# A fused attention and two-layer kernel: weight splits of layer 1 moved from GpSimd to ScalarE and VectorE, a buffer of its own for parked weights, and sums written from PSUM straight to x's two parts

## The chip, the cores and the metric

The kernel runs on one core of a Trainium2 chip. The metric is device time in microseconds (us) of one execution; lower is better. Before the change, three runs gave 705.80, 707.14 and 709.77 us, median 707.14. The core has five engines that run side by side, each in its own program order: TensorE (PE in the profile, its weight loads PEld), VectorE (DVE), ScalarE (ACT), GpSimd (POOL) and SyncE (SP), which here issues the DMAs.

## The reference, cut to what matters

```python
def reference(q, k, v, w_pre, w_post, moe_*, moe2_*):      # 2 x 12 heads x 448 x 64
    x = attention with head mixing before and after softmax  # -> [896, 768]
    h = x @ w_in                       # layer 1: [896, 768] @ [768, 2048]
    g = h * clip(h + 3, 0, 6) / 6
    x = g @ w_out                      # [896, 2048] @ [2048, 768]
    h = x @ w_in2                      # layer 2, the same sizes
    P = a0 + a1*h + a2*h^2 + a3*h^3
    Q = 1 + |b0|*|h| + |b1|*h^2
    return (P / (Q + 1e-6)) @ w_out2   # [896, 768]
```

[...]

## The kernel before, in words

**Exactness by splitting.** Every factor of a product is split in two float32r parts, a high part (rounded to what TensorE multiplies) and a low part (the rest): x = xh + xl, w = wh + wl. One product is then three matmuls, wh·xh, wh·xl and wl·xh, added up in the same PSUM bank (`mm3`, lines 387 to 389). Much of what the other engines do is to make these parts.

**Stages.** First the attention, whose order is written out by hand. Then layer 1's first product, called h here: 16 values of f (128 columns of w_in each), for each f two parts of the tokens (384 and 512 columns, `PARTS`), 6 x 3 matmuls each. `act1` makes g from h: ScalarE t (L561), VectorE g (L563), ScalarE the high part gh (L565), VectorE the low part gl (L566). Then layer 1's second product, called y: 6 blocks c of 128 rows; each needs all 16 gh and gl, and w_out in three units of 6, 6 and 4 values of f (`KSP`); two PSUM banks for a block, out of eight. At a block's end ScalarE copies y/6 from PSUM to a temporary buffer (L775), VectorE rounds it to XH (L776) and subtracts for XL (L777). XH and XL are the x of layer 2. Layer 2 is built alike, with other act functions. From the end of layer 1's first steps on (line 723) a scheduler sets the order on each engine, from the order of the code and from when it takes buffers to come free.

**Weights, unit by unit.** `advance` loads raw weights up to two units ahead (SP's queue, L426, into two wraw buffers) and splits one unit ahead. `split_pieces` takes a unit through: ScalarE scales the upper halves to float (L435), VectorE shifts (L437), puts in the sign (L439) and the lower bits (L443); this gives wf, of which there are two buffers. Then the high part wh and the low part wl, three buffers each. For the units of layer 1 ("in1" and "out1") GpSimd makes both (L459, L460); for those of layer 2 ScalarE makes wh (L462) and VectorE wl (L463).

**Parked weights.** For ten values of f of layer 2's w_in (2 to 11), `pre_slot` does the conversion already during layer 1 and parks the result in DRAM. It takes turns of three slots: load raw (L744), convert (into a wf buffer, with the same four steps L435 to L443), store (L752). Layer 2 later only loads the float (L411).

Of the kernel before, what the change touches and what calls it, by code (L numbers as in the profile page):

```python
# [7 lines left out]
F32 = mybir.dt.float32  # L8
F32R = mybir.dt.float32r
I32 = mybir.dt.int32  # L10
AF = mybir.ActivationFunctionType
ALU = mybir.AluOpType
# [36 lines left out]
def fused_kernel(  # L49
# [15 lines left out]
    nc = tc.nc  # L65
# [44 lines left out]
    XH = xp.tile([128, KD, NT], F32R, name="xh")  # L110
    XL = xp.tile([128, KD, NT], F32R, name="xl")
# [49 lines left out]
    for i, w in enumerate((w_pre, w_post)):  # L161
        nc.sync.dma_start(
            out=wrep[:, i, :], in_=w[None, :, :].to_broadcast([GR, H, H])
# [220 lines left out]
    pools = {}  # L384

    def mm3(o, wh, wl, mh, ml, first, last):
        nc.tensor.matmul(o, lhsT=wh, rhs=mh, start=first, stop=False)  # L387
        nc.tensor.matmul(o, lhsT=wh, rhs=ml, start=False, stop=False)  # L388
        nc.tensor.matmul(o, lhsT=wl, rhs=mh, start=False, stop=last)  # L389

    KSP = [(0, 6), (6, 12), (12, 16)]
    units = [("in1", f, 0) for f in range(KF)]
# [55 lines left out]
    def split_pieces(u):  # L448
        t, n = raws.pop(u)
        n *= 128  # L450
        if u[0] == "in2" and u[1] in pre:
            w = t
        else:
            w = pools["late"].tile([128, KD * 128], F32, tag="wf", bufs=2, name="wf")[:, :n]
            yield from to_f32(t, n, w)
        hv = pools["late"].tile([128, KD * 128], F32R, tag="wh", bufs=3, name="wh")[:, :n]
        lv = pools["late"].tile([128, KD * 128], F32R, tag="wl", bufs=3, name="wl")[:, :n]
        if u[0] in ("in1", "out1"):
            nc.gpsimd.tensor_scalar(out=hv, in0=w, scalar1=1.0, scalar2=0.0, op0=ALU.mult, op1=ALU.add)  # L459
            nc.gpsimd.tensor_tensor(out=lv, in0=w, in1=hv.bitcast(F32), op=ALU.subtract)  # L460
        else:
            nc.scalar.activation(out=hv, in_=w, func=AF.Copy)  # L462
            nc.vector.tensor_tensor(out=lv, in0=w, in1=hv.bitcast(F32), op=ALU.subtract)  # L463
        if u[0] == "out2":
            for d, x in zip(wsp[u[1]], (hv, lv)):
                nc.sync.dma_start(out=d, in_=x.bitcast(F32))
        else:
            hv, lv = (x.rearrange("p (a b) -> p a b", b=128) for x in (hv, lv))
        spl[u] = (hv, lv)
# [15 lines left out]
    def advance(i, ahead=2):  # L485
        load_units(i + ahead)
        split_units(i + 1)
# [60 lines left out]
            pass  # L548

    def tmp(name, n):  # L550
        return pools["gp"].tile([128, 512], F32, tag="tmp", bufs=4, name=name)[:, :n]

    def act1(f, p):
        t0, t1 = PARTS[p]
# [157 lines left out]
    gp = pools["gp"] = tc.alloc_tile_pool(name="gp", bufs=1, reuse_waits="tile")  # L712
# [15 lines left out]
    def bank(name):  # L728
        return pm.tile([128, 512], F32, tag="mm", name=name)
# [3 lines left out]
    slot, held = [0], {}  # L733

    def pre_slot():
        i, k = divmod(slot[0] - 1, 3)
        slot[0] += 1
        if not 0 <= i < len(PRE2):
            return
        f = PRE2[i]  # L740
        n = KD * 128
        if k == 0:
            held["t"] = gp.tile([128, 2 * n], I32, tag="wpre", name=f"wpre{f}")
            nc.sync.dma_start(  # L744
                out=held["t"].rearrange("p (a b) -> p a b", b=256), in_=w2i[:, :, f * 256 : f * 256 + 256]
            )
        elif k == 1:
            held["w"] = pools["late"].tile([128, n], F32, tag="wf", bufs=2, name="wf")
            for _ in to_f32(held["t"], n, held["w"]):
                pass  # L750
        else:
            nc.sync.dma_start(out=pre[f], in_=held["w"])  # L752
# [9 lines left out]
    for c in range(KD):  # L762
        hp = [bank(f"y1_{c}_{p}") for p in range(2)]
        for kk, (k0, k1) in enumerate(KSP):
            advance(ui)
            wh, wl = spl.pop(("out1", c, kk))
            for f in range(k0, k1):
                for p, (t0, t1) in enumerate(PARTS):
                    mm3(hp[p][:, : t1 - t0], wh[:, f - k0, :], wl[:, f - k0, :], gh[f][:, t0:t1], gl[f][:, t0:t1],
                        f == 0, f == KF - 1)  # L770
            pre_slot()
            ui += 1
        for p, (t0, t1) in enumerate(PARTS):
            y = tmp("y", t1 - t0)
            nc.scalar.activation(out=y, in_=hp[p][:, : t1 - t0], func=AF.Copy, scale=1.0 / 6.0)  # L775
            nc.vector.tensor_copy(out=XH[:, c, t0:t1], in_=y)  # L776
            nc.vector.tensor_tensor(out=XL[:, c, t0:t1], in0=y, in1=XH[:, c, t0:t1].bitcast(F32), op=ALU.subtract)  # L777
    pm.release()
    gp.release()

# [2 lines left out]
    gp = pools["gp2"] = tc.alloc_tile_pool(name="gp2", bufs=1, reuse_waits="tile")  # L783
# [57 lines left out]
    for f in range(KF):  # L841
        advance(ui, AHEAD2)
        w = spl.pop(("in2", f, 0))
# [8 lines left out]
        hp = hps[0]  # L852
        run(gemms[0])
        t1 = tm("t1", P0)
# [3 lines left out]
        if f == 0:  # L858
            hp = hps[1]
            run(gemms[1])  # L860
        else:
            hp = bank2(tags[1], f"h2_{f}_1")
# [55 lines left out]
    for t in range(NB0):  # L918
        o = gp.tile([TB, DM], F32, tag="o", bufs=3, name=f"o0_{t}")
# [15 lines left out]
    for t in range(NB1):  # L935
        row = P0 + t * TB
        o = gp.tile([TB, DM], F32, tag="o", bufs=3, name=f"o1_{t}")
# [61 lines left out]
```

## Time and profile before

| what | us |
|---|---|
| median of three runs | 707.14 |
| the profiled execution's own time | 707.37 |
| its span, first to last instruction | 705.7 |
| TensorE busy | 689.6 |
| VectorE busy | 557.2 |
| ScalarE busy | 411.1 |
| GpSimd busy | 256.9 |
| mean granted TensorE clock | 0.998 of full speed |

All rows below come from that one profiled execution; it lies within the three runs. Times in it count from the start of the span. A busy TensorE is one with a matmul on the way; matmuls overlap, so two starts can be closer together than a matmul is long. What TensorE really takes for a matmul is read from one start to the next.

### The profile page before, as it was taken

How to read it: one execution, taken by the hardware profiler on the slowest of the kernel's cores; microseconds unless marked ns; L12 is line 12 of the kernel's file. 1: busy time of each engine (PE TensorE's matmuls, PEld its weight loads, DVE VectorE, ACT ScalarE, POOL GpSimd, SP SyncE). 2: the span in 40 equal slices, each digit the busy share in tenths (PEclk: the TensorE clock that was granted, in tenths of full speed). 3: DMA queues.
4: the chain of work that ended last, by engine and by line, in shares of the span. 5: the costliest groups of instructions: out<-in, count | busy, mean ns of one | idle time of the engine just before them, and what ended most of it. 6: DMA issues, size and time to landing. Idle time of an engine off the chain costs nothing.

```text
span 705.7 us, 12410 instructions
## 1 busy us (share of the span) xinstructions
PE 689.6 (98%) x4461; PEld 617.5 (88%) x4461; DVE 557.2 (79%) x934; ACT 411.1 (58%) x851; POOL 256.9 (36%) x255
## 2 busy tenths in 40 slices
PE   8989999999999999999999999999999999999997
PEld 4768888888889888989888888889999999999997
DVE  6845585665657689889987777879999899989991
ACT  6757887887787343434342212227766667679851
POOL 2876775877776334323434543410000000000000
PEclk9999999999999999999999999999999999999999
DMA  5636486545394444555345544466575584755522
GB/s 206 226 111 176 142 209 190 166 142 166 119 260 123 148 144 136 155 157 156 121 151 177 186 160 141 140 247 236 209 270 186 196 267 144 242 196 202 188 82 89
DMA packets 76032, 122.81 MB, mean 174 GB/s; under 512 B 6804, under 2 KB 56260, under 8 KB 75972
## 3 DMA queue, kind: packets, MB, share of 16 engines
q1 hardware_dynamic: 75684, 121.66, 53.9%
q8 instruction: 35, 0.57, 0.3%
q10 hardware_dynamic: 288, 0.37, 0.1%
q14 instruction: 25, 0.20, 0.1%
HBM read 83.39 MB, written 19.27 MB: 145 GB/s over the span
## 4 chain that ended last, share of the span: by engine, by line
PE 60%; DVE 24%; DMA 7%; ACT 4%; issue 4%; POOL 0%; POOLq 0%; SPq 0%; ACTq 0%; DVEq 0%
PE A L341 9%; DVE wf L439 6%; PE h L389 6%; PE h L388 6%; PE h L387 6%; DVE wf L443 6%; PE acc L387 6%; PE acc L389 6%; PE acc L388 6%; PE X L363 5%; DMA pre<-wf 4%; PE sc L271 4%; DVE gl L566 4%; PE M L306 3%; DVE wf L437 3%
## 5 line engine op out<-in xcount | busy, mean ns | idle before, releaser
L389 PE MATMUL h<-xh,wl 128*128 128x512 f32 (+1 forms) x384 | 139.9, 364 | 0.8 <-DVE wl L463 0.8
L388 PE MATMUL h<-xl,wh 128*128 128x512 f32 (+1 forms) x384 | 139.5, 363 | 0.0
L387 PE MATMUL h<-xh,wh 128*128 128x512 f32 (+1 forms) x384 | 139.5, 363 | 0.0
L435 ACT ACTIVATE wf<-wraw 128x768 f32<-128x768 f32 (+1 forms) x56 | 48.7, 878 | 96.0 <-DMA pre<-wf 57.2
L296 POOL TENSOR_TENSOR sl<-full,sh 120x448 fp32r<-120x448 f32 x87 | 99.9, 1148 | 7.2
L310 DVE TENSOR_REDUCE st<-M 120x1 f32<-120x448 f32 x90 | 56.1, 623 | 51.3 <-PE M L308 51.1
L341 PEld LDWEIGHTS A<-wr,e 120*112 120x112 f32 x720 | 87.2, 178 | 7.9 <-ACT wr L325 3.9
L341 PE MATMUL A<-wr,e 120*112 120x120 f32 x720 | 89.7, 268 | 2.2 <-ACT wr L325 2.2
L459 POOL TENSOR_SCALAR wh<-wf 128x768 fp32r<-128x768 f32 (+1 forms) x34 | 32.6, 959 | 141.4 <-DVE wf L443 140.5
L312 ACT ACTIVATE e<-M,st 120x448 f32<-120x448 f32 x90 | 57.1, 635 | 42.7 <-DVE st L310 37.1
L389 PEld LDWEIGHTS h<-xh,wl 128*128 128x128 f32 x384 | 72.0, 188 | 9.0 <-DVE wl L463 1.1
L387 PEld LDWEIGHTS h<-xh,wh 128*128 128x128 f32 x384 | 72.1, 188 | 7.5
L388 PEld LDWEIGHTS h<-xl,wh 128*128 128x128 f32 x384 | 72.1, 188 | 7.6
L389 PE MATMUL y<-gh,wl 128*128 128x384 f32 x192 | 70.1, 365 | 2.6 <-POOL wl L460 2.6
L388 PE MATMUL y<-gl,wh 128*128 128x384 f32 x192 | 70.2, 366 | 1.0 <-DVE gl L566 1.0
L294 POOL TENSOR_SCALAR sh<-full 120x448 fp32r<-120x448 f32 x87 | 54.3, 624 | 46.1 <-PE M L307 21.5
L387 PE MATMUL y<-gh,wh 128*128 128x384 f32 x192 | 69.9, 364 | 0.0
L460 POOL TENSOR_TENSOR wl<-wf,wh 128x768 fp32r<-128x768 f32 (+1 forms) x34 | 67.5, 1985 | 2.8
L439 DVE SCALAR_TENSOR_TENSOR wf<-wraw,icst,wf 128x768 int32<-128x768 int32 (+1 forms) x56 | 61.7, 1103 | 0.7
L437 DVE TENSOR_SCALAR wf<-wf 128x768 int32<-128x768 int32 x66 | 43.1, 654 | 22.6 <-ACT wf L435 22.3
L443 DVE SCALAR_TENSOR_TENSOR wf<-wraw,icst,wf 128x768 int32<-128x768 int32 (+1 forms) x56 | 57.7, 1032 | 0.6
L565 ACT ACTIVATE gh<-g 128x384 fp32r<-128x384 f32 (+1 forms) x32 | 18.5, 579 | 60.3 <-DVE g L563 60.0
(114 smaller groups left out, 1521.7 us busy)
## 6 DMA issues: line engine op xcount, KB each, us to landing
wraw<-in_moe_w_out_dram SPq DMA_DIRECT2D x28, 768.0 KB
wraw<-in_moe_w_in_dram SPq DMA_DIRECT2D x22, 768.0 KB
full<-stg SPq DMA_DIRECT2D x60, 210.0 KB
vraw<-in_v_dram SPq DMA_DIRECT2D x42, 224.0 KB
wpre<-in_moe_w_in_dram SPq DMA_DIRECT2D x10, 768.0 KB
w2h<-wh SPq DMA_DIRECT2D x16, 384.0 KB
w2l<-wl SPq DMA_DIRECT2D x16, 384.0 KB
ws<-w2h SPq DMA_DIRECT2D x16, 384.0 KB
```

Of the source, the lines that this page charges most:

```text
L294: eng.tensor_scalar(out=sh[:r], in0=s[:r], scalar1=1.0, scalar2=0.0, op0=ALU.mult, op1=ALU.add)
L296: return lambda: eng.tensor_tensor(out=sl[:r], in0=s[:r], in1=sh[:r].bitcast(F32), op=ALU.subtract)
L310: nc.vector.tensor_reduce(out=st[:r, 0:1], in_=mt[:r, :S], op=ALU.max, axis=AX.X, negate=True)
L312: nc.scalar.activation(out=e[:r], in_=mt[:r, :S], func=AF.Exp, bias=st[:r, 0:1], accum_out=st[:r, 1:2])
L341: nc.tensor.matmul(av[:, jc], lhsT=e[:r, jc * JP : (jc + 1) * JP], rhs=wr[:r, :, :rr], start=True, stop=True)
L387: nc.tensor.matmul(o, lhsT=wh, rhs=mh, start=first, stop=False)
L388: nc.tensor.matmul(o, lhsT=wh, rhs=ml, start=False, stop=False)
L389: nc.tensor.matmul(o, lhsT=wl, rhs=mh, start=False, stop=last)
L437: nc.vector.tensor_scalar(out=wi, in0=wi, scalar1=3, scalar2=None, op0=ALU.logical_shift_left)
L439: nc.vector.scalar_tensor_tensor(out=wi, in0=hw, scalar=icst[:, 0:1], in1=wi, op0=ALU.bitwise_and, op1=ALU.bitwise_or)
L443: nc.vector.scalar_tensor_tensor(out=wi, in0=lw, scalar=icst[:, 1:2], in1=wi, op0=ALU.logical_shift_right, op1=ALU.bitwise_or)
L460: nc.gpsimd.tensor_tensor(out=lv, in0=w, in1=hv.bitcast(F32), op=ALU.subtract)
```

## The change

Three things. Units of layer 1 other than the first four (`units[:4]`, which are split during the end of the attention) are split by ScalarE and VectorE, as those of layer 2. Parked weights are converted in a buffer of their own, wfp, and the temporary buffers of `act1` go from four to three. And at the end of a block of y, ScalarE writes y/6 from PSUM to XH itself, rounding on the way, and VectorE makes XL with one operation, PSUM times 1/6 minus XH.

```diff
-        if u[0] in ("in1", "out1"):
+        if u in units[:4]:
             nc.gpsimd.tensor_scalar(out=hv, in0=w, scalar1=1.0, scalar2=0.0, op0=ALU.mult, op1=ALU.add)
             nc.gpsimd.tensor_tensor(out=lv, in0=w, in1=hv.bitcast(F32), op=ALU.subtract)
         else:
...
     def tmp(name, n):
-        return pools["gp"].tile([128, 512], F32, tag="tmp", bufs=4, name=name)[:, :n]
+        return pools["gp"].tile([128, 512], F32, tag="tmp", bufs=3, name=name)[:, :n]
...
         elif k == 1:
-            held["w"] = pools["late"].tile([128, n], F32, tag="wf", bufs=2, name="wf")
+            held["w"] = gp.tile([128, n], F32, tag="wfp", name="wfp")
             for _ in to_f32(held["t"], n, held["w"]):
                 pass
...
         for p, (t0, t1) in enumerate(PARTS):
-            y = tmp("y", t1 - t0)
-            nc.scalar.activation(out=y, in_=hp[p][:, : t1 - t0], func=AF.Copy, scale=1.0 / 6.0)
-            nc.vector.tensor_copy(out=XH[:, c, t0:t1], in_=y)
-            nc.vector.tensor_tensor(out=XL[:, c, t0:t1], in0=y, in1=XH[:, c, t0:t1].bitcast(F32), op=ALU.subtract)
+            y, o = hp[p][:, : t1 - t0], XH[:, c, t0:t1]
+            nc.scalar.activation(out=o, in_=y, func=AF.Copy, scale=1.0 / 6.0)
+            nc.vector.scalar_tensor_tensor(
+                out=XL[:, c, t0:t1], in0=y, scalar=1.0 / 6.0, in1=o.bitcast(F32), op0=ALU.mult, op1=ALU.subtract
+            )
```

The scheduler then moves instructions. The first place is VectorE in the h stage, around f = 9 (names with h_9 belong to it; wfp is the parked weight). Before:

```order
L437 TENSOR_SCALAR wf<-wf 128x768
L566 TENSOR_TENSOR gl_4010<-g_4038,gh_4009 128x512
L439 SCALAR_TENSOR_TENSOR wf<-wraw,icst,wf 128x768
L563 SCALAR_TENSOR_TENSOR g_4077<-t_4075,h_9_0_4054 128x384
L443 SCALAR_TENSOR_TENSOR wf<-wraw,icst,wf 128x768
L566 TENSOR_TENSOR gl_4074<-g_4077,gh_4073 128x384
L437 TENSOR_SCALAR wf<-wf 128x768
L439 SCALAR_TENSOR_TENSOR wf<-wraw,icst,wf 128x768
L443 SCALAR_TENSOR_TENSOR wf<-wraw,icst,wf 128x768
L563 SCALAR_TENSOR_TENSOR g_4102<-t_4100,h_9_1_4081 128x512
L566 TENSOR_TENSOR gl_4074<-g_4102,gh_4073 128x512
```

Here VectorE converts two weights one after the other between the gl's, and makes no wl. The same place in the change:

```order
L437 TENSOR_SCALAR wf<-wf 128x768
L566 TENSOR_TENSOR gl_4010<-g_4038,gh_4009 128x512
L439 SCALAR_TENSOR_TENSOR wf<-wraw,icst,wf 128x768
L563 SCALAR_TENSOR_TENSOR g_4077<-t_4075,h_9_0_4054 128x384
L443 SCALAR_TENSOR_TENSOR wf<-wraw,icst,wf 128x768
L566 TENSOR_TENSOR gl_4074<-g_4077,gh_4073 128x384
L437 TENSOR_SCALAR wfp<-wfp 128x768
L439 SCALAR_TENSOR_TENSOR wfp<-wpre_4639,icst,wfp 128x768
L463 TENSOR_TENSOR wl<-wf,wh 128x768
L563 SCALAR_TENSOR_TENSOR g_4102<-t_4100,h_9_1_4081 128x512
L443 SCALAR_TENSOR_TENSOR wfp<-wpre_4639,icst,wfp 128x768
L566 TENSOR_TENSOR gl_4074<-g_4102,gh_4073 128x512
```

A wl has come in, and the sixth parked weight (wpre_4639), which before was converted in the first block of y.

The second place is VectorE at the end of the first block of y (y_0_0 and y_0_1 are its two banks). Before:

```order
L439 SCALAR_TENSOR_TENSOR wf<-wpre_4639,icst,wf 128x768
L443 SCALAR_TENSOR_TENSOR wf<-wpre_4639,icst,wf 128x768
L437 TENSOR_SCALAR wf<-wf 128x512
L439 SCALAR_TENSOR_TENSOR wf<-wraw,icst,wf 128x512
L437 TENSOR_SCALAR wf<-wf 128x768
L443 SCALAR_TENSOR_TENSOR wf<-wraw,icst,wf 128x512
L439 SCALAR_TENSOR_TENSOR wf<-wraw,icst,wf 128x768
L443 SCALAR_TENSOR_TENSOR wf<-wraw,icst,wf 128x768
L776 CAST xh<-y 128x384
L776 CAST xh<-y 128x512
L777 TENSOR_TENSOR xl<-y,xh 128x384
L777 TENSOR_TENSOR xl<-y,xh 128x512
```

The same place in the change:

```order
L443 SCALAR_TENSOR_TENSOR wf<-wraw,icst,wf 128x768
L463 TENSOR_TENSOR wl<-wf,wh 128x768
L437 TENSOR_SCALAR wf<-wf 128x512
L439 SCALAR_TENSOR_TENSOR wf<-wraw,icst,wf 128x512
L443 SCALAR_TENSOR_TENSOR wf<-wraw,icst,wf 128x512
L463 TENSOR_TENSOR wl<-wf,wh 128x768
L437 TENSOR_SCALAR wf<-wf 128x768
L439 SCALAR_TENSOR_TENSOR wf<-wraw,icst,wf 128x768
L443 SCALAR_TENSOR_TENSOR wf<-wraw,icst,wf 128x768
L776 SCALAR_TENSOR_TENSOR xl<-y_0_0_4502,xh 128x384
L463 TENSOR_TENSOR wl<-wf,wh 128x512
L776 SCALAR_TENSOR_TENSOR xl<-y_0_1_4503,xh 128x512
```

No parked weight is left here; the two wl of 768 columns for the next block stand ahead of the block's xl.

The third place is SP's queue from the end of h into y (pre is a store of a parked weight, wpre a load of the next). In the change:

```order
L744 DMA wpre_4925<-in_moe_w_in_dram 128x6x256
L426 DMA wraw<-in_moe_w_out_dram 128x6x256
L426 DMA wraw<-in_moe_w_out_dram 128x4x256
L752 DMA pre_76<-wfp 128x768
L744 DMA wpre_5068<-in_moe_w_in_dram 128x6x256
L426 DMA wraw<-in_moe_w_out_dram 128x6x256 x2
L752 DMA pre_77<-wfp 128x768
L744 DMA wpre_5211<-in_moe_w_in_dram 128x6x256
L426 DMA wraw<-in_moe_w_out_dram 128x4x256
L752 DMA pre_78<-wfp 128x768
L426 DMA wraw<-in_moe_w_out_dram 128x6x256 x2
```

Before, pre_76 to pre_78 stood among the loads of y's last blocks, each three weight loads from the next; now all ten are through by the time the second block's weights are loaded.

## Rows read from the trace of the kernel before

**Rows 1.** The page's first part: span, and busy time of each engine.

```profile
span 705.7 us, 12410 instructions
PE 689.6 (98%) x4461; PEld 617.5 (88%) x4461; DVE 557.2 (79%) x934; ACT 411.1 (58%) x851; POOL 256.9 (36%) x255
```

**Rows 2.** Table by stretch (h, y, layer 2): length; PE, PEld, DVE, ACT, POOL; clock, DMA, GB/s.

```profile
230.00:346.00 116.00, 116.00 (x648) 103.58 (x648) 99.38 (x112) 46.76 (x77) 42.32 (x29) 1.00 0.49 148
346.00:468.00 122.00, 118.45 (x581) 104.28 (x579) 100.45 (x106) 30.33 (x46) 51.44 (x34) 1.00 0.51 167
468.00:706.00 238.00, 232.97 (x1247) 220.39 (x1246) 210.47 (x327) 157.63 (x264) 0.00 (x0) 1.00 0.56 193
```

**Rows 3.** TensorE's waits: who waited for whom, us in total, times, longest.

```profile
PE y L389 <- POOL wl L460: 2.6, 5, 0.8
...
PE y L388 <- DVE gl L566: 1.0, 1, 1.0
PE h L389 <- DVE wl L463: 0.8, 1, 0.8
```

**Rows 4.** TensorE's timeline, y and the start of layer 2: start, duration, instruction.

```profile
346.48 0.34 PE L387 MATMUL y<-gh,wh 128*128 128x384 f32 x1
...
347.00 0.39 PE L387 MATMUL y<-gh,wh 128*128 128x512 f32 x1
...
360.97 0.34 PE L387 MATMUL y<-gh,wh 128*128 128x384 f32 x1
...
421.73 0.34 PE L388 MATMUL y<-gl,wh 128*128 128x384 f32 x1
422.88 0.44 PE L389 MATMUL y<-gh,wl 128*128 128x384 f32 x1 [0.81 <-POOL wl L460]
...
467.58 0.34 PE L387 MATMUL h<-xh,wh 128*128 128x384 f32 x1
...
469.18 0.34 PE L387 MATMUL h<-xh,wh 128*128 128x384 f32 x1
```

**Rows 5.** ScalarE's waits within the stretch 346 to 468 (y).

```profile
ACT wf L435 <- DMA pre<-wf: 50.3, 6, 10.2
ACT wf L435 <- DMA wraw<-in_moe_w_out_dram: 13.7, 3, 5.2
```

**Rows 6.** VectorE's and GpSimd's timelines in h, without and with each other.

```profile
258.99 0.69 DVE L566 TENSOR_TENSOR gl<-g,gh 128x512 fp32r<-128x512 f32 x1 [0.23 <-ACT gh L565]
...
276.42 2.03 POOL L460 TENSOR_TENSOR wl<-wf,wh 128x768 fp32r<-128x768 f32 x1
276.67 2.33 DVE L566 TENSOR_TENSOR gl<-g,gh 128x512 fp32r<-128x512 f32 x1
```

**Rows 7.** Groups by line and shape: count, busy us and mean ns, idle time before.

```profile
L439 DVE SCALAR_TENSOR_TENSOR wf<-wraw,icst,wf 128x768 int32<-128x768 int32 x50 | 57.2, 1145 | 0.5
L460 POOL TENSOR_TENSOR wl<-wf,wh 128x768 fp32r<-128x768 f32 x28 | 56.9, 2031 | 2.3
...
L566 DVE TENSOR_TENSOR gl<-g,gh 128x512 fp32r<-128x512 f32 x16 | 26.2, 1640 | 4.9 <-ACT gh L565 4.9
...
L463 DVE TENSOR_TENSOR wl<-wf,wh 128x768 fp32r<-128x768 f32 x22 | 21.0, 954 | 2.0 <-ACT wh L462 1.8
...
L462 ACT ACTIVATE wh<-wf 128x768 fp32r<-128x768 f32 x22 | 18.7, 848 | 14.3 <-PE h L388 6.6 <-DVE wf L443 5.3 <-DMA w2l<-wl 1.9
...
L777 DVE TENSOR_TENSOR xl<-y,xh 128x384 fp32r<-128x384 f32 x6 | 9.9, 1652 | 0.0
```

**Rows 8.** VectorE's timeline in h, a stretch in which GpSimd is idle.

```profile
272.00 0.55 DVE L437 TENSOR_SCALAR wf<-wf 128x768 int32<-128x768 int32 x1
272.47 0.54 DVE L563 SCALAR_TENSOR_TENSOR g<-t,h 128x384 f32<-128x384 f32 x1
272.94 1.00 DVE L439 SCALAR_TENSOR_TENSOR wf<-wraw,icst,wf 128x768 int32<-128x768 int32 x1
273.87 0.55 DVE L566 TENSOR_TENSOR gl<-g,gh 128x384 fp32r<-128x384 f32 x1
```

## The prediction

> **What bounds the kernel now.** I read the page's busy line first. TensorE is busy 98% of the span, VectorE 79%, GpSimd 36% [rows 1]. A TensorE that is busy 98% leaves little: whatever the change does on the other engines can only return the time in which TensorE stood still. So the question is how long it stands still near the changed lines, and why.
>
> The table by stage splits the span at the points where layer 1's first product (h), its second product (y) and layer 2 begin [rows 2]. TensorE is busy all 116 us of h, 118.45 of the 122 us of y, 232.97 of the 238 us of layer 2. The granted clock is 1.00 in all three, the upper level of 2.4 GHz, so no time hangs on the clock.
>
> The list of TensorE's waits names what ended the idle time [rows 3]: GpSimd's wl five times (2.6 us), VectorE's gl once (1.0), VectorE's wl once (0.8). The first two lie in y, the third at the start of layer 2. The timeline prices these stops more fully, because a stop also spoils the overlap of the matmul behind it [rows 4]. One value of f in y (six matmuls) takes (360.97 - 346.48)/12 = 1.2075 us, start to start. The stage has 6 blocks of 16 of them, so 96 x 1.2075 = 115.9 us undisturbed. It takes 467.58 - 346.48 = 121.1: **5.2 us are lost in y**. Layer 2's first three matmuls take 469.18 - 467.58 = 1.60 where three of the same width take 0.52 (346.48 to 347.00): **1.1 us** more. The largest single stop is at 421.73: 1.15 us to the next start, not 0.17. The list names no other stop of TensorE in layer 2.
>
> Why is GpSimd late? The list of ScalarE's waits in y says so [rows 5]: ScalarE waits 50.3 us, six times, for the store "pre<-wf", before it may start to convert the next weights. The parked weights of layer 2 sit in one of only two wf buffers until the store has landed, and ScalarE, VectorE and GpSimd queue up behind it. Then the work comes in a bunch, where GpSimd and VectorE hold each other up: beside GpSimd's wl of 2.03 us, VectorE's gl of 512 columns, which 18 us before took 0.69, took 2.33 [rows 6].
>
> **The change part by part.**
>
> *Parked weights get their own buffer (wfp).* The store then holds up only the next parked conversion, not a weight that TensorE waits for. The 50.3 us of ScalarE's wait in y go; ScalarE has the room, 30.3 us busy of 122 [rows 2]. The scheduler reacts: the order shows all ten parked conversions in the h stage, where five stood before and five in y. So h gets 5 x 3 more VectorE operations (one shift, two of the L439 kind) and y loses them. It also gets five more loads of 768 KB and stores of 384 KB, 5.9 MB in all: 148 GB/s x 116 us = 17.2 MB become 23.1, or 199 GB/s. The DMA engines carried 148 GB/s with a share of 0.49 [rows 2], so I put the share at 0.66: covered. SP's queue issues in order, and each parked load now stands behind a store that waits for VectorE's last wfp step; behind it stands the next weight load. That load has a unit of 7.2 us in hand.
>
> *Splits by ScalarE and VectorE, not GpSimd.* 30 units (12 of in1, 18 of out1) lose a GpSimd pair and gain one ScalarE copy (848 ns at 768 columns) and one VectorE subtraction (954 ns) [rows 7]. From the finished wf to the finished wl that is about 1.8 us, where GpSimd needed 2.03 for the wl alone, after its own wh. GpSimd then does nothing after unit 4, so the holding-up goes: gl at 512 columns, 1640 ns on the mean over 16 [rows 7], should come down to about 690, and L439, 1145 on the mean, to about 1000.
>
> *VectorE in h is the place to be careful.* Start to start, undisturbed, a shift takes 0.47 us, g and gl at 384 columns 0.47 each, an L439 0.93 [rows 8]; g and gl at 512 columns about 0.61 (0.69 against 0.55 for the two widths of gl [rows 6, 8]), wl about 0.87 (0.954 less the 0.08 by which neighbours overlap). For one f: 0.47 + 2 x 0.93 + 0.87 + 2 x (0.47 + 0.61) = 5.36. The ten parked conversions add 2.33 each over 14 values of f: 1.66. Together **7.0 us**, where TensorE needs 6 x 1.2075 = 7.245. That is the lower end of the cost. The upper end takes every operation at its full duration, 0.08 more for each of 8 + 3 x 10/14 operations: 7.8. I take the lower end, since the order puts independent operations between the steps of one weight, as in rows 8. At 7.0 TensorE waits for nothing; even a little over, weights stand ready a unit ahead (three wh and wl buffers), and y wants the last gl only at f = 15, some 18 us into its first block. In y VectorE needs per block 2 x (0.47 + 1.86 + 0.87) + 2.1 for the short unit (two thirds of a long one) + 1.1 for x = 9.6 of 19.3 us: nothing.
>
> *x straight from PSUM.* Twelve VectorE casts go, a copy and a subtraction from SBUF become ScalarE's scaled write and one VectorE operation with a PSUM operand; the subtraction alone, held up as it was, took 1652 ns at 384 columns [rows 7]. The new operation resembles L563, which also reads PSUM and one SBUF operand and takes 0.54 us at that width [rows 8]. Both stand off the path: layer 2 begins with the other five row blocks of x and has about 6 us before it needs the last one. The bank is held longer by one operation, under a microsecond, and eight banks rotate two per block. Cost: nothing. One temporary buffer fewer (three, not four) delays ScalarE's t only if the gl two steps back is late; at 7.0 us per f it is not. Cost: nothing, and 0.1 to 0.2 us per f if VectorE falls behind (that lies in the rival below).
>
> *The sum.* The profiled execution took 707.37 us: a span of 705.7 and 1.67 around it; it is 0.2 above the median of the three runs shown (707.14). The attention part is the same instructions: 0. Stops of TensorE in y: -5.2. The stop at layer 2's start: -1.1. New stops: 0. 707.4 - 6.3 = **701.1 us**.
>
> *A rule against the change.* VectorE's instruction count rises by 18 (30 subtractions more, 12 casts fewer), and in h the window's 99.4 us of VectorE work [rows 2] would become, if nothing got shorter, 99.4 + 14 x 0.954 + 5 x 2.55 = 125.5 us in 116. The Trainium skill ("VectorE: DVE Perf Modes", Rules for kernel authors) says to lower the number of VectorE operations, since each pays its own drain; by that alone the change makes h longer, and this is the slower rival below. The rows speak for the other reading: much of the 99.4 is waiting for GpSimd, as 2.33 against 0.69 shows [rows 6]. The Trainium skill ("SBUF — State Buffer", Who interferes with whom) has that too: a VectorE operation with two SBUF inputs and a GpSimd operation that reads SBUF exclude each other for the whole instruction. With this the sum is the one above.
>
> **The rivals.**
> 1. *Half comes back* (chance 0.10). TensorE's stops in y are ended by weights, and in y ScalarE also waited 13.7 us for raw loads [rows 5]. If loads are what arrives last once the store is out of the way, TensorE waits for VectorE's wl where it waited for GpSimd's. Against it: y now has ten transfers of parked weights fewer. With half of each stop left: 707.4 - 3.1 = 704.2.
> 2. *The change does nothing* (0.08). y ends 6.3 us sooner, but layer 2's VectorE is busy 210.5 us of 238 and its weights come through the same rings; if layer 2's pace is set there, it gives the gain back in stops that do not exist now. Against it: 11% of VectorE is idle there, and its weights were parked earlier. Time: 707.
> 3. *VectorE becomes the bound in h: slower* (0.08). Price from above: 125.5 - 116 = 9.5 us of TensorE waiting for wl or gl, the 6.3 still gained: 707.4 - 6.3 + 9.5 = 710.6. By the upper end of my own count it is 14 x (7.8 - 7.245) = 7.8, so 708.9. It turns slower than before once VectorE spends more than 7.245 + 6.3/14 = 7.7 us per f.
>
> **How the numbers follow.** The forecast has 0.74, the rivals 0.26. A measurement of this kernel can tell about 0.5%, 3.5 us, from no change: faster means below 703.6. The forecast lies 6 us below the median, and the three runs spread from 1.3 below to 2.6 above it. Faster: all of the forecast's chance and four tenths of rival 1: 0.78. Slower by over 0.5%, above 710.7: half of rival 3 and a little for what I do not see: 0.05. The rest, 0.17, is within. The range goes from 701.1 less the runs' 1.3 and a little for stops too small to list, 699.5, to the half gain plus as much, 705.5; outside lie rivals 2 and 3.
>
> **What would show it.** Right: TensorE's waits in y and at the start of layer 2 gone; y's stage at 116 us; VectorE's gl at 512 columns near 690 ns and L439 near 1000; no idle time of ScalarE before L435 that ended with the store; h still without a stop and 115 to 116 us long. Wrong: TensorE waiting for wl L463 or gl L566 within h, VectorE's share there above 97%; a stop at layer 2's weights; or y's waits still there, with a raw load as what ended them.

## The result and the profile after

| | before | after |
|---|---|---|
| median of the runs | 706.77 us (4 runs, 705.8 to 709.77) | 699.54 us (4 runs, 699.18 to 701.36) |
| ratio, with its 95% interval | | 0.9896 [0.9861, 0.993] |
| profiled execution (span) | 707.37 (705.7) | 701.36 (699.6) |

The change makes the kernel 7.2 us faster by the medians, where 6.3 were forecast. 699.5 is the very low end of the range; by the ratio, 0.9896 x 706.77 = 699.4, it is a tenth of a microsecond beyond it. The four runs before are the three of the section above and a fourth of 706.41 us.

The page of the changed kernel: span and busy time of each engine, then the chain of work that ended last. The rows to set beside them are [rows 1].

```profile
span 699.6 us, 12328 instructions
PE 687.2 (98%) x4460; PEld 618.0 (88%) x4461; DVE 531.0 (76%) x952; ACT 434.1 (62%) x881; POOL 167.4 (24%) x195
...
PE 93%; DMA 3%; DVE 2%; ACT 2%; issue 0%; POOL 0%; SPq 0%; POOLq 0%; DVEq 0%; ACTq 0%
```

The chain of the kernel before:

```profile
PE 60%; DVE 24%; DMA 7%; ACT 4%; issue 4%; POOL 0%; POOLq 0%; SPq 0%; ACTq 0%; DVEq 0%
```

VectorE runs 18 more instructions (952, not 934) and is busy 26 us less (531.0, not 557.2). The chain moved with it: before, 24% of it ran over VectorE and 7% over transfers; now 93% is TensorE itself. These shares tell where the chain ran and not what is gained, which is read from the stages below.

The table by stretch of the changed kernel, with the columns of [rows 2] (h, y, layer 2):

```profile
231.00:347.40 116.40, 116.40 (x652) 104.19 (x652) 105.37 (x150) 64.68 (x102) 5.19 (x4) 1.00 0.64 198
347.40:463.20 115.80, 115.80 (x577) 103.99 (x576) 67.46 (x90) 36.34 (x52) 0.00 (x0) 1.00 0.40 136
463.20:700.00 236.80, 232.98 (x1249) 220.66 (x1247) 208.72 (x323) 156.68 (x263) 0.00 (x0) 1.00 0.55 188
```

TensorE is now busy all through y. GpSimd is busy 5 us in h, where it had 42, and not at all in y, where it had 51; VectorE's work in y falls from 100 to 67 us, in h it rises from 99 to 105. The list of TensorE's waits, of which [rows 3] are the counterpart, has no entry left in h, y or layer 2. Its longest are now all in the attention part:

```profile
PE M L306 <- POOL sh L294: 3.0, 1, 3.0
PE A L341 <- ACT wr L325: 2.2, 4, 0.9
...
PE X L363 <- DMA vraw<-in_v_dram: 1.1, 1, 1.1
```

Groups by line and shape of the changed kernel, to be read beside [rows 7]:

```profile
L439 DVE SCALAR_TENSOR_TENSOR wf<-wraw,icst,wf 128x768 int32<-128x768 int32 x50 | 51.4, 1029 | 0.8
L463 DVE TENSOR_TENSOR wl<-wf,wh 128x768 fp32r<-128x768 f32 x46 | 45.5, 988 | 34.6 <-ACT wh L462 34.6
L462 ACT ACTIVATE wh<-wf 128x768 fp32r<-128x768 f32 x46 | 38.8, 843 | 63.6 <-PE y L388 45.2 <-PE h L388 10.5 <-DVE wf L443 5.5
L566 DVE TENSOR_TENSOR gl<-g,gh 128x512 fp32r<-128x512 f32 x16 | 11.0, 687 | 0.0
...
L776 DVE SCALAR_TENSOR_TENSOR xl<-y,xh 128x384 fp32r<-128x384 f32 x6 | 3.3, 551 | 3.1 <-ACT xh L775 3.1
```

The same 16 instructions gl at 512 columns take 687 ns instead of 1640. ScalarE's wh (the third row) now waits mostly for TensorE to free a buffer (45.2 of 63.6 us): the weights are ready ahead of time.

To see where the time went I take the starts of the first matmul of each stage from TensorE's timeline. "Attention" is all that comes ahead of h, and h is counted from its first matmul behind the attention's last product (a few matmuls of h stand among the attention's and count with it); "tail" is all behind the start of the last matmul:

| us | attention | h | y | layer 2 | tail | span |
|---|---|---|---|---|---|---|
| before | 234.60 | 111.88 | 121.10 | 233.86 | 4.26 | 705.7 |
| after | 235.77 | 111.60 | 115.86 | 232.61 | 3.76 | 699.6 |
| difference | +1.17 | -0.28 | -5.24 | -1.25 | -0.50 | -6.1 |

The bounds of three of the columns, in the changed kernel's timeline (start of y, last matmul of y, last matmul of all):

```profile
347.37 0.34 PE L387 MATMUL y<-gh,wh 128*128 128x384 f32 x1
...
463.00 0.39 PE L389 MATMUL y<-gh,wl 128*128 128x512 f32 x1
...
695.84 0.34 PE L389 MATMUL acc<-ws,xl 128*128 128x384 f32 x1
```

### The profile page after: what moved, and what is told of

Read it like the earlier page. It is cut to its first block, busy times and chain, and to the rows that moved or that the text cites. A ratio compares the mean times of both kernels' runs of the same rounds, so it can differ in the third digit from the quotient of the medians.

```text
span 699.6 us, 12328 instructions
## 1 busy us (share of the span) xinstructions
PE 687.2 (98%) x4460; PEld 618.0 (88%) x4461; DVE 531.0 (76%) x952; ACT 434.1 (62%) x881; POOL 167.4 (24%) x195
## 4 chain that ended last, share of the span: by engine, by line
PE 93%; DMA 3%; DVE 2%; ACT 2%; issue 0%; POOL 0%; SPq 0%; POOLq 0%; DVEq 0%; ACTq 0%
PE h L388 11%; PE h L389 11%; PE h L387 11%; PE A L341 9%; PE acc L387 6%; PE acc L389 6%; PE acc L388 6%; PE y L388 6%; PE y L387 6%; PE y L389 5%; PE X L363 5%; PE sc L271 4%; PE M L306 3%; PE M L308 2%; PE M L307 2%; DMA vraw<-in_v_dram 2%
## 5 line engine op out<-in xcount | busy, mean ns | idle before, releaser
L462 ACT ACTIVATE wh<-wf 128x768 fp32r<-128x768 f32 (+1 forms) x52 | 42.6, 818 | 63.6 <-PE y L388 45.2
L463 DVE TENSOR_TENSOR wl<-wf,wh 128x768 fp32r<-128x768 f32 (+1 forms) x52 | 49.5, 953 | 34.6 <-ACT wh L462 34.6
L443 DVE SCALAR_TENSOR_TENSOR wf<-wraw,icst,wf 128x768 int32<-128x768 int32 (+1 forms) x56 | 56.5, 1010 | 0.7
L439 DVE SCALAR_TENSOR_TENSOR wf<-wraw,icst,wf 128x768 int32<-128x768 int32 (+1 forms) x56 | 55.9, 999 | 1.0
L348 ACT ACTIVATE at<-A 112x480 f32<-112x480 f32 x87 | 50.3, 578 | 1.8 <-PE A L341 1.8
L306 PE MATMUL M<-sh,wp_h 120*120 120x448 f32 x90 | 41.0, 456 | 3.0 <-POOL sh L294 3.0
```

The costliest lines, as they stand in the source:

```text
L306: nc.tensor.matmul(mt[:r, :S], lhsT=a[:r, :r], rhs=sh[:r], start=True, stop=False)
L348: aposts.append(lambda: nc.scalar.activation(out=o, in_=av, func=AF.Copy))
L439: nc.vector.scalar_tensor_tensor(out=wi, in0=hw, scalar=icst[:, 0:1], in1=wi, op0=ALU.bitwise_and, op1=ALU.bitwise_or)
L443: nc.vector.scalar_tensor_tensor(out=wi, in0=lw, scalar=icst[:, 1:2], in1=wi, op0=ALU.logical_shift_right, op1=ALU.bitwise_or)
```

## The experiments

Two theories stood against each other. **A**: GpSimd's splits are the cause; taking them off GpSimd is the gain. It has two forms: A1, VectorE and GpSimd hold each other up, so that VectorE's results are late; A2, GpSimd's own 2 us a weight are too slow. **B**: the store of the parked weights holds the wf buffers, so that everything queues up behind it; the own buffer is the gain. As the prediction had it, B made GpSimd late and A1 did the rest. The experiments took the change apart, then loaded what it had emptied. (Raw weights, wraw and wpre in the rows, are the 64-bit values as they lie in DRAM, read as pairs of 32-bit integers.)

All stages in one table, read as above. The stages are those of the profiled execution, the times medians, the ratios against the kernel before on the same chip, with their 95% interval. The rows come from three chips, on which the kernel before had medians of 707.39 us (the first four rows), 707.22 (VectorE loaded once and the two with gathers) and 708.31 (the other four); rows of different chips are compared by their ratios:

| kernel | attention | h | y | layer 2 | time, us | ratio |
|---|---|---|---|---|---|---|
| own buffer alone | 235.77 | 111.61 | 122.72 | 232.84 | 707.52 | 1.0011 [0.999, 1.0032] |
| splits alone | 233.98 | 111.61 | 115.85 | 232.80 | 699.13 | 0.9888 [0.9844, 0.9932] |
| x from PSUM alone | 232.46 | 111.88 | 117.78 | 232.91 | 702.95 | 0.9933 [0.9901, 0.9964] |
| buffer and PSUM | 235.24 | 111.60 | 123.16 | 232.63 | 708.25 | 0.9999 [0.9973, 1.0025] |
| splits and PSUM | 233.62 | 111.61 | 115.85 | 232.61 | 698.70 | 0.9873 [0.9834, 0.9912] |
| buffer and splits | 234.19 | 111.60 | 115.85 | 232.82 | 699.46 | 0.988 [0.9834, 0.9927] |
| useless GpSimd work | 235.64 | 111.60 | 127.34 | 232.96 | 711.78 | 1.006 [1.0037, 1.0083] |
| VectorE loaded once | 234.10 | 111.61 | 115.85 | 232.63 | 700.48 | 0.9894 [0.9859, 0.9929] |
| VectorE loaded twice | 233.26 | 127.14 | 116.34 | 232.62 | 714.84 | 1.01 [1.0041, 1.016] |
| gathers on ScalarE's queue | 240.84 | 111.61 | 115.85 | 232.63 | 706.20 | 0.9985 [0.9964, 1.0006] |
| the same, other order | 240.93 | 111.61 | 115.85 | 232.63 | 706.67 | 0.9978 [0.996, 0.9995] |

### The three parts, each alone

Own buffer for the parked weights, with the three temporary buffers that make room for it:

```diff
-        return pools["gp"].tile([128, 512], F32, tag="tmp", bufs=4, name=name)[:, :n]
+        return pools["gp"].tile([128, 512], F32, tag="tmp", bufs=3, name=name)[:, :n]
-            held["w"] = pools["late"].tile([128, n], F32, tag="wf", bufs=2, name="wf")
+            held["w"] = gp.tile([128, n], F32, tag="wfp", name="wfp")
```

> The kernel before with the parked weights' own buffer alone (and three temporary buffers); GpSimd still splits, x still goes through the temporary buffer. Theory A (GpSimd is the cause: its splits are long, and while one runs VectorE's operations with two SBUF inputs stand still): the buffer alone does little, the y stage stays at 119 to 121 us (before 121.1, undisturbed 115.9), TensorE still waits for wl L460, time within 2 us of before. Theory B (the buffer is the cause: the store holds one of two wf buffers for 50 us of y): y falls to 117 or less, time 4 to 6 us below before, though GpSimd still works.

The splits without GpSimd, nothing else:

```diff
-        if u[0] in ("in1", "out1"):
+        if u in units[:4]:
```

> The kernel before with layer 1's splits on ScalarE and VectorE alone; the parked weights still take a wf buffer until their store has landed. Theory A: y at 116 to 117 us and the stop at the start of layer 2 gone, time 5.5 to 7 us below before, that is nearly all of the change's gain; ScalarE's wait for the store stays in tens of us and costs nothing. Theory B: the store still holds the weights up, y at 119 us or more, gain 2 us at most.

The last part of the diff alone (x's two parts straight from PSUM, lines 774 to 778 of the changed kernel):

> The kernel before with x written straight from PSUM alone. Both theories: it takes work off VectorE at block ends but leaves GpSimd and the store, y at 119.5 to 121 us, time within 1.5 us of before. A third theory, C (the casts and subtractions of x, 1.25 and 1.65 us each, are what delays wl): y at 118 or less and 3 us gained.

**Measured.** The splits alone are the whole change: 0.9888, y 115.85 us, where it takes 115.9 undisturbed. The buffer alone gives nothing (1.0011), and y is even 1.6 us longer than before. ScalarE's waits within y, of the kernel with the buffer alone:

```profile
ACT wf L435 <- POOL wl L460: 43.6, 9, 6.6
ACT wf L435 <- DMA wraw<-in_moe_w_out_dram: 21.8, 6, 6.7
```

and of the kernel with the splits alone, in which the store still holds wf as it did before:

```profile
ACT wh L462 <- PE y L388: 43.6, 12, 6.4
...
ACT wf L435 <- DMA pre<-wf: 1.0, 4, 0.3
```

So theory B falls as the account of the gain: the splits alone bring all of it. The 50.3 us that ScalarE waited for the store [rows 5] are gone in both; that they would stay with the splits alone, as the expectation had it, was a miss. With the buffer they come back as 43.6 us of waiting for GpSimd's wl; without the buffer, but without GpSimd too, they become 43.6 us of waiting for TensorE, which is slack. ScalarE was waiting for whatever happened to end last in a stage in which it had little to do. With x from PSUM alone the wait even stays, and TensorE's stops for wl all but go. ScalarE's longest wait in y, and the table by stretch for y's last four blocks, of that kernel:

```profile
ACT wf L435 <- DMA pre<-wf: 46.7, 6, 9.7
```

```profile
381.00:462.00 81.00, 81.00 (x404) 72.48 (x403) 54.62 (x60) 18.20 (x26) 36.01 (x23) 1.00 0.54 175
```

TensorE is busy all of these 81 us, with 36.1 us of the waiting for the store and 36.0 of GpSimd's work in them.

Why the buffer is no help with GpSimd still at work shows in TensorE's waits of that kernel (h, y and layer 2):

```profile
PE y L388 <- DVE gl L566: 1.8, 2, 1.6
PE y L387 <- DVE g L563: 1.1, 1, 1.1
PE y L387 <- ACT gh L565: 0.6, 1, 0.6
PE y L389 <- POOL wl L460: 0.4, 1, 0.4
```

TensorE's stops for GpSimd's wl fall from 2.6 us [rows 3] to 0.4, as the buffer was to bring, and not as theory A expected. But the scheduler moves the parked conversions forward, beside GpSimd: eight of the ten run in h and two at the start of y, where before four ran in h and six in y. VectorE's operations are held up there; so g, gh and gl are late for y's first block. Groups of the kernel with the buffer alone:

```profile
L439 DVE SCALAR_TENSOR_TENSOR wfp<-wpre,icst,wfp 128x768 int32<-128x768 int32 x10 | 16.2, 1618 | 0.3
...
L566 DVE TENSOR_TENSOR gl<-g,gh 128x512 fp32r<-128x512 f32 x16 | 17.9, 1116 | 0.4 <-ACT gh L565 0.4
```

The parked L439 takes 1618 ns there and 1043 in the changed kernel, where GpSimd is still. All of the 6.9 us that y loses lie in its first 28 us. About 1.7 of them are matmuls at a longer pitch: from 371 to 376 us the granted clock is 0.66, a part of the stretch at 1.2 GHz, after 4 us in which TensorE was busy 2 us. Behind that the buffer does what it was meant to. The table by stretch, and GpSimd's longest wait in the same stretch:

```profile
386.00:470.00 84.00, 84.00 (x419) 75.41 (x418) 46.92 (x57) 15.78 (x23) 30.96 (x22) 1.00 0.41 137
```

```profile
POOL wh L459 <- PE y L388: 33.2, 10, 5.2
```

TensorE is busy all 84 us (before, 82.19 of the 84.6 from 383 us to the end of y), and GpSimd is so far ahead that it waits for TensorE to free a buffer. So in this kernel the stops in y's later blocks came when three things met: GpSimd's splits, parked weights converted and stored during y, and x's casts and subtractions at the end of a block. Each part of the change takes one of them away, and any one ends nearly all of these stops (0.2 us of waiting for wl is left with PSUM, 0.4 with the buffer). Only the splits also end the late gl in y's first block, and so bring the whole gain. Whether it is the store's hold or the parked conversions themselves that count in the second isn't separated.

x straight from PSUM is worth 4.4 us by itself (0.9933), where I had put it at nothing; the expectation's third theory, C, came out. Groups of that kernel:

```profile
L460 POOL TENSOR_TENSOR wl<-wf,wh 128x768 fp32r<-128x768 f32 x28 | 56.7, 2025 | 2.3
L566 DVE TENSOR_TENSOR gl<-g,gh 128x512 fp32r<-128x512 f32 x16 | 26.3, 1642 | 4.9 <-ACT gh L565 4.9
...
L776 DVE SCALAR_TENSOR_TENSOR xl<-y,xh 128x384 fp32r<-128x384 f32 x6 | 3.3, 546 | 0.0
```

gl and wl are as slow as before [rows 7]; what is gone is the x operation that collided with GpSimd: 546 ns, where the subtraction took 1652, and the cast ahead of it is gone as well. TensorE's stops for wl in y fall from 2.6 us to 0.2, and y from 121.10 to 117.78. That agrees with the same cause, met by a part of the change that I had judged by its instructions alone; once GpSimd is off, the same edit brings nothing (the pairs, below).

### The parts in pairs

> The change with GpSimd still making the splits of layer 1: buffer and direct write together. Theory A: y at 118 us or more, TensorE still waits for wl L460, gain at most 3 us. Theory B: y at 116 to 117, gain 5 to 6.5 us, so the split's engine would not matter.

> The change without the parked weights' own buffer: splits on ScalarE and VectorE, x straight from PSUM. Theory A (taking GpSimd off is the whole gain): as the splits alone, y at 115.9 us, 7 to 8 us below before, within 1 us of the whole change. If the buffer still matters beside the splits (what is left of theory B): y at 117 or more, 2 us or more above the whole change.

> The change without the direct write: splits and buffer, x through the temporary buffer. Theory A: y at 115.9 us, within 1 us of the whole change. If the direct write carries part of the gain also without GpSimd: y at 116.5 or more.

**Measured.** Both pairs with the splits have y at 115.85 and no stop of TensorE from h on; the third pair, with buffer and PSUM but GpSimd at work, has 123.16 and is no faster than before (0.9999). The parts don't add up: with GpSimd at work, PSUM gives 4.4 us and the buffer takes that back (708.25 against 702.95); with GpSimd off, neither gives anything that can be measured. The splits with PSUM and without the buffer, the fastest median at 698.70, have an interval that overlaps those of the splits alone and of the whole change: as good as these, and with less code than the latter.

### Useless work on GpSimd

Splits and PSUM, and beside each split a subtraction on GpSimd whose result nobody reads:

```diff
             nc.vector.tensor_tensor(out=lv, in0=w, in1=hv.bitcast(F32), op=ALU.subtract)
+            if u[0] in ("in1", "out1"):
+                d = pools["gp"].tile([128, KD * 128], F32, tag="decoy", name="decoy")[:, :n]
+                nc.gpsimd.tensor_tensor(out=d, in0=gh[0][:, :n].bitcast(F32), in1=hv.bitcast(F32), op=ALU.subtract)
```

> Splits on ScalarE and VectorE and the direct write, with a useless GpSimd subtraction of the same size beside each of the 30 units (it reads wh and a finished gh, writes a buffer that nobody reads). No TensorE operand comes from GpSimd. Theory A1 (GpSimd did harm by shutting VectorE out): gl of 512 columns goes back up to 1300 ns or more, h or y get stops again, y at 117 us or more, at least 2 us slower than the same kernel without the decoy. Theory A2 (GpSimd did harm by its own length, since wl came out of it): VectorE gets slower, but TensorE does not wait, y stays at 116 and the time within 1 us.

**Measured.** This parts A1 from A2: nothing of TensorE waits for GpSimd's result in h and y here. y is 11.5 us longer (127.34 against 115.85), and what TensorE stops for is VectorE's wl:

```profile
PE y L389 <- DVE wl L463: 8.5, 9, 2.0
```

Groups of this kernel over the whole span, the useless subtraction among them:

```profile
L466 POOL TENSOR_TENSOR decoy<-gh,wh 128x768 f32<-128x768 f32 x24 | 61.5, 2564 | 109.2 <-ACT wh L462 109.2
L463 DVE TENSOR_TENSOR wl<-wf,wh 128x768 fp32r<-128x768 f32 x46 | 58.7, 1276 | 3.2 <-ACT wh L462 3.1
...
L569 DVE TENSOR_TENSOR gl<-g,gh 128x512 fp32r<-128x512 f32 x16 | 12.5, 779 | 1.6 <-ACT gh L568 1.6
```

VectorE's groups within y:

```profile
L443 DVE SCALAR_TENSOR_TENSOR wf<-wraw,icst,wf 128x768 int32<-128x768 int32 x12 | 23.8, 1986 | 0.2
L443 DVE SCALAR_TENSOR_TENSOR wf<-wpre,icst,wf 128x768 int32<-128x768 int32 x6 | 13.4, 2238 | 0.2
```

The same in y without the useless work (splits and PSUM):

```profile
L443 DVE SCALAR_TENSOR_TENSOR wf<-wraw,icst,wf 128x768 int32<-128x768 int32 x12 | 12.2, 1014 | 0.2
...
L443 DVE SCALAR_TENSOR_TENSOR wf<-wpre,icst,wf 128x768 int32<-128x768 int32 x5 | 5.1, 1019 | 0.2
```

The useless subtraction meets whatever VectorE does behind a split: in h it is wl, 1276 ns on the mean of all 46 where it takes 955 without; in y it is the last step of the next weight's conversion (L443), 1986 and 2238 ns instead of 1014 and 1019, some 19 us of VectorE in y. The rest of what VectorE has more in y (100.4 us busy against 72.2) is work that came over from h: one parked conversion, and g and gl of two more values of f. So A1 needs no A2: GpSimd instructions that no one waits for cost 11.5 us of TensorE. The place where it shows was missed: gl at 512 columns stays at 779, because it doesn't fall beside the subtraction. A2 is not excluded by this as a part of the old loss (five of the old stops were ended by GpSimd's own wl), but it isn't needed, and by the kernel with the buffer alone GpSimd's 2 us a weight are fast enough.

One thing came back with the useless work. ScalarE's longest wait in y:

```profile
ACT wf L435 <- DMA pre<-wf: 25.9, 5, 6.4
```

Without the useless work it is 0.9 us. Whether the held wf buffers carry a part of the 11.5 us is open: useless work beside the own buffer wasn't run.

### How much VectorE can take in h

The changed kernel, with gl's subtraction (0.47 + 0.61 = 1.08 us per f) written twice, and three times:

```diff
         nc.vector.tensor_tensor(out=gl[f][:, t0:t1], in0=g, in1=o.bitcast(F32), op=ALU.subtract)
+        nc.vector.tensor_tensor(out=gl[f][:, t0:t1], in0=g, in1=o.bitcast(F32), op=ALU.subtract)
```

> The whole change with VectorE's gl made twice in h, 1.08 us more per f: the second point on VectorE's slack. With four to five parked conversions left in h the count is 5.36 + 1.08 + 0.8 = 7.2 us per f, TensorE needs 7.245. With the slack that the whole change showed (VectorE 105.4 us busy of 116.4): no stop in h, h at 111.6 to 112, time within 1.5 us of the whole change. If the rival's threshold of 7.7 us per f is too high: stops in h, 2 us or more.

> The whole change with VectorE's gl made three times over in h, 2.16 us more of VectorE per f, to find where VectorE becomes the bound (the slower rival). The own count gives 5.36 + 2.16 = 7.52 us per f without the parked weights, 9.2 with all ten in h; TensorE needs 7.245. If the rival's price is right: h stops, 4 to 25 us longer than 111.6, the wait named is VectorE's gl or wl, and the time goes above before. If there is more slack than counted: h within 1 us of 111.6.

**Measured.** Once more costs nothing: h 111.61, 700.48 us. Twice more makes h 15.5 us longer (127.14) and the kernel slower than before (1.01). TensorE's waits of the latter, and its table by stretch for h:

```profile
PE h L387 <- ACT wh L462: 7.8, 3, 4.4
...
PE h L389 <- DVE wl L463: 1.2, 2, 0.8
```

```profile
236.00:360.00 124.00, 114.98 (x536) 100.28 (x535) 119.71 (x189) 59.83 (x92) 2.67 (x2) 0.96 0.41 125
```

VectorE is busy 119.7 of 124 us, 97%, where the changed kernel has 105.37 of 116.40, 91%. The third rival is thus real, and some way off. The expectation named gl or wl as what TensorE would wait for; mostly it is ScalarE's wh, but the largest part of ScalarE's own waits in h is for VectorE's g (26.2 us). My count of VectorE's time for one f fits both kernels, once one sees that the scheduler reacts: it leaves five parked conversions in h with one more gl, and four with two more, where the change has nine. So 5.36 + 1.08 + 5 x 2.33/14 = 7.27 us per f in the first, against TensorE's 7.245, a loss of 14 x 0.03 = 0.4 us at most, and none was measured; and 5.36 + 2.16 + 4 x 2.33/14 = 8.19 in the second, 14 x (8.19 - 7.245) = 13.2 us of loss, where 15.5 were measured. The clock may be a part of the rest: 0.96 granted in that stretch, some of it at 1.2 GHz, where h of the changed kernel has 1.00.

### A try at the attention's stop

After the change the longest stop left is the 3.0 us for sh in the attention part, which hangs on a gather transfer. SP's queue issues the gathers one after the other, so I sent three of them from ScalarE's queue (on top of splits and PSUM); in a second kernel I also changed the order of the heads that have to wait for them (the table ONES):

```diff
-        nc.sync.dma_start(out=to[:, : chunks[C][3]], in_=st[: chunks[C][3] * GR])
+        eng = nc.scalar if C == 1 and h < 2 * FIRST and h % 2 == 0 else nc.sync
+        eng.dma_start(out=to[:, : chunks[C][3]], in_=st[: chunks[C][3] * GR])
```

```diff
-    ONES, BYV = [1, 3, 5], (5, 7, 9)
+    ONES, BYV = [1, 2, 3], (5, 7, 9)
```

> A version that aims below both kernels: splits on ScalarE and VectorE, direct write, and three of the attention's gather transfers for the second chunk (even heads of its first six) issued from ScalarE's queue, not SP's. In every trace so far TensorE stops 0.7 to 3.0 us at 36 to 40 us for GpSimd's sh, which waits for these transfers, and SP issues one about every 0.8 us from 11.8 to 32.8. If SP's issuing is what makes them late, they land some 2.4 us sooner, the stop goes, and the attention ends at 231 to 232.5 instead of 232.5 to 235.8: 1 to 3 us gained, about 696. If the transfers themselves are the limit, or ScalarE's issuing delays its own copies: no gain, or up to 2 us lost.

> As the run beside it, and the second chunk's last three pairs of scores are computed in steps 1, 2 and 3 of the first chunk, not 1, 3 and 5. If the transfers wait for the scores, they are issued 2 to 4 us sooner and the stop goes for certain: 1 to 3 us below the splits with the direct write. If SP or the transfers are the limit: as the run beside it, within 1 us; steps that are fuller could cost up to 1 us.

**Measured.** Worse by some 8 us than splits and PSUM without it (0.9985 against 0.9873), which neither outcome of the expectation had, and the order of the heads changes nothing (0.9978). ScalarE's timeline at that place, in the first of the two, and TensorE's longest wait:

```profile
12.66 1.40 ACTq L253 DMA_DIRECT2D full<-stg  x1
...
21.16 2.55 ACTq L253 DMA_DIRECT2D full<-stg  x2
...
23.75 1.04 ACT L293 ACTIVATE sh<-full 120x448 fp32r<-120x448 f32 x2 [8.68 <-DMA full<-stage]
```

```profile
PE M L307 <- ACT sh L293: 8.1, 1, 8.1
```

The three issues take 0.8 to 1.4 us each of ScalarE's own queue, and sh, which ScalarE makes, comes behind them: it starts at 23.75 us, after 8.68 us without work, and TensorE stands 8.1 us. With splits and PSUM alone ScalarE starts its first sh at 15.61. The profile names a gather of SP's queue (full<-stage) as what ended the idle time; it landed within 0.02 us of the end of ScalarE's last issue, so which of the two held sh up isn't settled. The granted clock of 20 to 30 us is 0.54 there (1.2 GHz for most of it, while TensorE is busy 5.62 of the 10 us); in the changed kernel it is 1.00 in those 10 us. Whether a gather sent from another queue would help wasn't tried.

## Why the prediction was right, and where it was wrong

Forecast were 701.1 us and 6.3 us gained, measured 699.5 and 7.2. The two priced stops came out. Two steps failed: the paragraph that made the store the origin of the loss, and, in the sum, the zero for everything outside these stops.

**Stops in y, forecast -5.2: right**, measured -5.24. The same loss was read from the pitch of an undisturbed f (1.2075 us) and not from the list of waits, which named 3.6 us of it.

**Stop at layer 2's start, forecast -1.1: right**, -1.25 over the whole of layer 2.

**"Why is GpSimd late? The list of ScalarE's waits in y says so": wrong.** This is the step that failed in the reasoning. The store did end ScalarE's idle time, but those 50.3 us were no measure of a loss: with the store left where it was and GpSimd taken off, all the gain is there; with the store left and x from PSUM, ScalarE waits 46.7 us for it and TensorE 0.2 us for wl; with the store out of the way and GpSimd at work, y's later blocks lose nothing, but the beginning of y 6.9 us. The parked weights in y were one of three things that had to meet there. All the gain hangs on another, that GpSimd and VectorE hold each other up; the second half of the same paragraph said that, and I made it the consequence. The sum came out near because the change had both parts. Had it been the buffer alone, the same reasoning would have forecast most of 6 us, and there is nothing.

**Cost of the splits: right.** gl at 512 columns 687 ns (forecast about 690), L439 1029 (about 1000). The Trainium skill ("VectorE: DVE Perf Modes", Rules for kernel authors) advises to keep the number of VectorE operations low. The trace disagrees for this case, with 18 operations more and 26 us less VectorE time. The 9.5 us that the slower rival put on h for these operations didn't come: h is 0.28 us shorter. The Trainium skill ("SBUF — State Buffer", Who interferes with whom) states that a VectorE instruction with two SBUF inputs contends with a GpSimd instruction that reads SBUF. The useless subtraction agrees: beside it VectorE's L443 takes 1986 ns instead of 1014, though no data passes between them.

**VectorE in h, forecast 7.0 us per f: near enough.** Busy 105.37 us of 116.40, or 6.6 of each 7.245. Nine of the ten parked conversions run in h and the tenth at the start of y, with 0.64 of the DMA engines' time and 198 GB/s (forecast 0.66 and 199), and h has no stop.

**x straight from PSUM, forecast nothing: right in this change only.** Alone it brings 4.4 us. I costed the operation (0.54 us forecast, 551 ns measured) but had judged the twelve casts and twelve subtractions harmless for lying off the path, though those of 384 columns take 1253 and 1652 ns apiece beside GpSimd and hold up what VectorE has to do next.

**All the rest, forecast 0: this is the mis-sized term, by 1.0 us**, and with the base it is why the time fell at the edge of the range. By the stages behind the attention, the change is worth 0.28 + 5.24 + 1.25 + 0.50 = 7.27 us, which is the 7.2 between the medians if the attention part, the same instructions, is taken as unchanged. I had 6.3, with no term for h and the tail: the h stage had a small stop (0.28 us at its end, 339.1 in the timeline) too short for the list to name, and the tail is 0.50 shorter, which I can't explain (3.76 to 3.84 us in the eight traces in which GpSimd has no work in h and y beyond the first units, 4.06 to 4.67 in the four with its splits). And the attention part, with the same instructions, ended between 232.46 and 235.77 us in the traces that leave it alone: the profiled execution of the changed kernel has nearly the worst of it, which is how it came to 701.36, the forecast's 701.1, by accident. The base was high as well: the profiled 707.37 is 0.6 above the median 706.77. These two, 1.0 of stages and 0.6 of base, are the 1.6 us between 701.1 and 699.5. The low end of the range allowed 1.3 us for the runs' spread and 0.3 for stops too small to list; those came to about 0.4 (0.28 in h, the rest in layer 2), and for the tail's 0.50 and the high base there was nothing.

**Rivals.** The first (loads arrive last) didn't come: with the splits alone ScalarE still waits 11.6 us for raw loads in y, and TensorE for none. The second (layer 2 gives it back) neither: layer 2 is itself 1.25 us shorter. The third isn't in this change, but it exists, as two more gl operations per f show.

## What to carry to other kernels

An idle time that ended with a store says what came last, not what it cost: look first at whether anyone waited for that engine, and if a change has several parts, forecast each one alone and beside the others: here any one of three ended the same stops, one of them brought new ones, and the gains didn't add up. Where one operation takes 0.69 us in one place and 2.33 in another, look for the neighbour that stretches it; here it did so even when nobody needed its result. Put the loss of a stage at its length less the undisturbed pitch times its count, over all stages, since small stops don't appear in the list of waits.

## What the hardware showed beyond that

The attention part varies by 3.3 us between executions of the same instructions. Most of it arises at TensorE's wait for sh at about 37 to 40 us, 0.7 us in the kernel with PSUM alone and 3.0 in the changed one; a second place is the wait for raw v (vraw), up to 1.4 us with the buffer alone and in no list with splits and PSUM. The first of them, in the changed kernel:

```profile
39.60 0.47 PE L306 MATMUL M<-sh,wp_h 120*120 120x448 f32 x1 [2.95 <-POOL sh L294]
```

Around the longer stop the clock is lower too, and that adds to it. Table by stretch for 36 to 46 us, of the changed kernel and of the kernel with PSUM alone:

```profile
36.00:46.00 10.00, 6.50 (x39) 5.47 (x39) 3.25 (x12) 3.57 (x11) 6.69 (x9) 0.83 0.35 98
```

```profile
36.00:46.00 10.00, 8.65 (x61) 6.71 (x60) 5.53 (x16) 5.82 (x17) 8.78 (x11) 1.00 0.38 106
```

The granted clock is 0.83 in the former, a part of the stretch at 1.2 GHz, and 1.00 in the latter, all of it at 2.4. Traces with a stop of 2.1 us there show either (1.00 with splits and PSUM, 0.83 with VectorE loaded once), so what decides between them stays open.
